# kv of two pairs of heads computed next to the q·kv of the two pairs ahead of them

## The chip, the cores and the metric

The kernel runs on one core of one Trainium2 chip. The metric is the time of one execution in microseconds (us), taken as the median of several runs. The granted clock is the share of its full clock that TensorE was given, averaged over a run.

## The reference, cut to what matters

```python
# q, k, v: (batch 8, heads 8, seq 576, head_dim 64), f32
kv  = einsum('bhsd,bhse->bhde', k, v)        # 64 x 64 for each head
out = einsum('bhsd,bhde->bhse', q, kv)
out = out / sqrt(mean(out * out, -1) + 1e-6) * g_norm
x = out.transpose(0, 2, 1, 3).reshape(4608, 512)
a, b = x @ w1, x @ w2                        # (512, 1024) each
result = ((a * b) @ w3) @ w_out              # (4608, 512)
```

## The kernel before

The kernel first folds w3 and w_out into one matrix (the first 85 us), and then runs nine groups of 512 tokens. In each, the FFN matmuls (all in a function `winograd`, 128 x 128 weights, 256 columns) fill TensorE, and the attention of the next batch is slipped in between them in pieces, at points called `between()`. There are up to eight such points, or stretches, in a group. The heads go in four pairs.

```python
inp = ctx.enter_context(tc.tile_pool(name="inp", bufs=2))          # k, v, q of two pairs
ps_at = ctx.enter_context(tc.tile_pool(name="ps_at", bufs=3, space=PSUM))
kv_sb = [const.tile([P, 2, NP, D], FP32, name=f"kv_sb{i}") for i in range(2)]
...
def kv(rs):                      # of pairs rs; one PSUM bank
    for r in rs:
        for j in range(J + 1):
            for e in range(2):   # 128 rows x 64 columns of the array
                nc.tensor.matmul(kv_ps[e * D:(e + 1) * D, r - rs[0], :], lhsT=..., rhs=..., ...)
    ...                          # four copies to kv_sb on ScalarE

def q_t(r):                      # 4 full-size transposes, one bank, one copy on ScalarE
def product(h):                  # q kv of pairs 2h, 2h+1: 64 x 64 tiles, two banks
    ...
    return norm(...)             # squares on ScalarE, sums, reciprocal and scaling on VectorE
def turn(r):                     # 4 full-size transposes of the result

def begin(*rs):
    kv(rs)
    for r in rs:
        q_t(r)
        load_pair(...)           # k, v and q of the pair two ahead

pieces = [
    [(begin, 0, 1)], [(middle, 0)], [(turn, 0), (turn, 1)],
    [(begin, 2, 3)], [(middle, 1)], [(turn, 2), (turn, 3)],
    [], [],                      # odd batches: leftover tokens of two batches
]
```

`middle(h)` is `product(h)` with its whole norm. The last 64 tokens of each batch, the leftovers, are treated two batches at a time, by `q_t_left`, `product_left` and `turn_left`.

## Time and profile before

| | before |
|---|---|
| median of the first 3 runs | 814.15 us (813.13 to 815.48) |
| span of the profiled run, granted clock | 811.6 us, 1.000 |
| TensorE / VectorE / ScalarE busy | 99% / 45% / 33% |
| TensorE's waits after 85 us | none |

The lines are shown in the prediction below. In a line of TensorE, `128*64` is the part of its array that the instruction uses, rows by columns; this is called the tile form here. TensorE's records overlap: an FFN matmul's record lasts 379 ns, and the next starts 216 ns after it. So a share of busy time says nothing of what one instruction costs on this path. Read the distance from one start to the next, and compare the same group of instructions with different neighbours.

### The profile page before, as it was taken

How to read it: one execution, taken by the hardware profiler on the slowest of the kernel's cores; microseconds unless marked ns; L12 is line 12 of the kernel's file. 1: busy time of each engine (PE TensorE's matmuls, PEld its weight loads, DVE VectorE, ACT ScalarE, POOL GpSimd, SP SyncE). 2: the span in 40 equal slices, each digit the busy share in tenths (PEclk: the TensorE clock that was granted, in tenths of full speed). 3: DMA queues.
4: the chain of work that ended last, by engine and by line, in shares of the span. 5: the costliest groups of instructions: out<-in, count | busy, mean ns of one | idle time of the engine just before them, and what ended most of it. 6: DMA issues, size and time to landing. Idle time of an engine off the chain costs nothing.

```text
span 811.6 us, 12588 instructions
## 1 busy us (share of the span) xinstructions
PE 803.0 (99%) x5335; PEld 676.8 (83%) x5335; DVE 363.6 (45%) x680; ACT 266.8 (33%) x501; POOL 1.8 (0%) x8
## 2 busy tenths in 40 slices
PE   7999999999999999999999999999999999999998
PEld 5455788888888888888888888888888888888887
DVE  6958998324522453155315531543154415422431
ACT  6677743124312431233124322331234212211220
POOL 0000000000000000000000000000000000000000
PEclk9999999999999999999999999999999999999999
DMA  9996433032003210312032202120210010002001
GB/s 322 332 328 182 146 91 92 1 131 82 10 1 130 75 31 1 119 47 56 1 103 67 66 1 85 56 82 0 79 52 1 1 52 1 0 1 53 1 0 53
DMA packets 60811, 59.53 MB, mean 73 GB/s; under 512 B 15316, under 2 KB 57300, under 8 KB 60756
## 3 DMA queue, kind: packets, MB, share of 16 engines
q1 hardware_dynamic: 60608, 58.60, 23.2%
q8 instruction: 42, 0.69, 0.4%
q14 instruction: 13, 0.11, 0.0%
q10 hardware_dynamic: 148, 0.13, 0.0%
HBM read 49.28 MB, written 9.44 MB: 72 GB/s over the span
## 4 chain that ended last, share of the span: by engine, by line
PE 98%; DMA 1%; DVE 0%; SPq 0%; ACT 0%; issue 0%; ACTq 0%
PE mm L471 81%; PE mm L456 7%; PE at L275 3%; PE at L345 2%; PE at L294 2%; PE at L378 2%; DMA raw<-in_moe_w_out_dram 1%; PE at L443 1%; PE at L363 0%; SPq L183 0%; PE at L387 0%; PE at L304 0%; DVE chunks L160 0%; DVE ab L150 0%; ACT ab L147 0%
## 5 line engine op out<-in xcount | busy, mean ns | idle before, releaser
L471 PE MATMUL mm<-xT,w_sb 128*128 128x256 f32 x768 | 176.2, 379 | 0.0
L471 PEld LDWEIGHTS mm<-xT,w_sb 128*128 128x128 f32 x768 | 146.0, 190 | 20.2 <-issue 0.5
L471 PE MATMUL mm<-xc,ws 128*128 128x256 f32 x576 | 130.2, 379 | 0.0
L471 PEld LDWEIGHTS mm<-xc,ws 128*128 128x128 f32 x576 | 109.5, 190 | 14.8
L484 ACT COPY u<-mm 128x512 f32<-128x512 f32 x90 | 52.7, 585 | 206.0 <-PE mm L471 185.9
L484 ACT COPY p<-mm 128x512 f32<-128x512 f32 x90 | 52.7, 586 | 134.4 <-PE mm L471 134.4
L471 PE MATMUL mm<-w3o_sb,ab 128*128 128x256 f32 x432 | 96.2, 379 | 0.0
L597 DVE TENSOR_TENSOR c<-mm,u 128x512 f32<-128x512 f32 x36 | 24.8, 689 | 157.3 <-PE mm L471 157.3
L471 PEld LDWEIGHTS mm<-w3o_sb,ab 128*128 128x128 f32 x432 | 82.1, 190 | 11.1
L471 PE MATMUL mm<-xc,w_sb 128*128 128x256 f32 x288 | 68.9, 382 | 0.0
L471 PE MATMUL mm<-raw 128*128 128x256 f32 x288 | 63.6, 379 | 0.0
L471 PE MATMUL mm<-xT,ws 128*128 128x256 f32 x256 | 61.6, 383 | 0.0
L471 PEld LDWEIGHTS mm<-raw 128*128 128x128 f32 x288 | 54.8, 190 | 7.4
L456 PE MATMUL mm<-chunks,ab 128*128 128x512 f32 x128 | 60.0, 601 | 0.2 <-DVE chunks L160 0.2
L471 PEld LDWEIGHTS mm<-xc,w_sb 128*128 128x128 f32 x288 | 52.8, 190 | 6.9 <-ACT u L484 0.3
L471 PEld LDWEIGHTS mm<-xT,ws 128*128 128x128 f32 x256 | 46.7, 190 | 6.0
L314 DVE TENSOR_REDUCE inv<-sq 128x8 f32<-128x512 f32 (+1 forms) x40 | 23.5, 626 | 58.4 <-ACT sq L313 58.4
L598 DVE TENSOR_TENSOR ab<-c 128x256 f32<-128x256 f32 x108 | 45.4, 421 | 2.9
L638 DVE TENSOR_TENSOR raw<-mm,u 128x512 f32<-128x512 f32 x8 | 5.5, 692 | 83.4 <-PE mm L471 72.7
L456 PEld LDWEIGHTS mm<-chunks,ab 128*128 128x128 f32 x128 | 21.9, 190 | 21.6 <-issue 16.1
L597 DVE TENSOR_TENSOR c<-p,u 128x512 f32<-128x512 f32 x36 | 24.9, 691 | 28.4 <-ACT u L484 28.1
L471 PE MATMUL mm<-w3o_sb,raw 128*128 128x256 f32 x144 | 32.7, 380 | 0.0
(90 smaller groups left out, 769.3 us busy)
## 6 DMA issues: line engine op xcount, KB each, us to landing
raw<-in_moe_w_dram SPq DMA_DIRECT2D x31, 512.0 KB, 7.0
k_sb<-in_k_dram SPq DMA_DIRECT2D x32, 256.0 KB, 3.9
v_sb<-in_v_dram SPq DMA_DIRECT2D x32, 256.0 KB, 4.4
q_sb<-in_q_dram SPq DMA_DIRECT2D x32, 256.0 KB, 4.5
out_dram<-raw SPq DMA_DIRECT2D x14, 512.0 KB, 2.6
raw<-in_moe_w_out_dram SPq DMA_DIRECT2D x7, 512.0 KB, 7.7
out_dram<-raw SPq DMA_DIRECT2D x9, 128.0 KB, 2.4
kl_sb<-in_k_dram SPq DMA_DIRECT2D x8, 128.0 KB, 4.8
```

Source lines behind the costliest of these rows:

```text
L275: nc.tensor.matmul(kv_ps[e * D:(e + 1) * D, r - rs[0], :], lhsT=k_sb[:, e, cols] if j < J else kl[:, 2 * r + e, :], rhs=v_sb[:, e, cols] i ...
L294: nc.tensor.transpose(qt_ps[:, e, i, :], q_sb[:, e, i * P:(i + 1) * P], ident)
L314: nc.vector.tensor_reduce(out=inv[:, i], in_=sq.rearrange("p (h d) -> p h d", d=D), axis=AX.X, op=ALU.add)
L345: nc.tensor.matmul(o_ps[l][tokens, n * D:(n + 1) * D], lhsT=qT[r][rows, e, i, tokens], rhs=kv_b[rows, e, r, :], start=True, stop=True,)
L378: nc.tensor.transpose(t_ps[:, j, :], st[r // 2][:, j // 2, j % 2, m:m + 2, :], ident)
L443: nc.tensor.transpose(t_ps[:, m, :], src, ident)
L456: nc.tensor.matmul(sums_ps[half][m], lhsT=w3T[half, c][:, m, :], rhs=chunks[:, c, 1, :], start=(c == 0), stop=(c == KF - 1),)
L471: nc.tensor.matmul(ps[:, u, :], lhsT=lhsT(a_name, u, c), rhs=rhs(b_name, c),  start=(u == 0 and c == 0 and to is None), stop=(c == chunks ...
L484: nc.scalar.copy(t, ps)
L597: nc.vector.tensor_add(c, one, two)
L598: nc.vector.tensor_mul(dst, c[:, 0, :], c[:, 1, :])
L638: nc.vector.tensor_add(dst, one, two)
```

## The change

The intent is to have fewer places where TensorE goes from full-size matmuls to small tiles and back. A border between two tile forms is called a seam here, and a place where kv is put directly next to a product a merge. kv(2,3) moves to the stretch of product(0), and kv(0,1) of the next batch to the stretch of product(1). As kv is now ready while the kv of two other batches is still needed (the leftovers use it), it gets a third place. Loads of k and v come apart from those of q. The core of the diff:

```diff
-    def load_pair(b, r):
+    def load_pair(names, b, r):
 ...
-        kv_b = kv_sb[b % 2]
+        kv_b = kv_sb[b % 3]
 ...
-                            rhs=kv_sb[l][rows, e, r, :],
+                            rhs=kv_sb[(b - 1 + l) % 3][rows, e, r, :],
 ...
-        def begin(*rs):
+        def begin_kv(*rs):
             kv(rs)
             for r in rs:
+                load_ahead("kv", r)
+
+        def begin_q(*rs):
+            for r in rs:
                 q_t(r)
 ...
-        pieces = [
-            [(begin, 0, 1)],
-            [(middle, 0)],
-            [(turn, 0), (turn, 1)],
-            [(begin, 2, 3)],
-            [(middle, 1)],
-            [(turn, 2), (turn, 3)],
-            [],
-            [],
-        ]
 ...
+        if b == 1:
+            fs[0].append((a.begin_kv, 0, 1))
+        fs[0].append((a.begin_q, 0, 1))
+        fs[1] += [(a.begin_kv, 2, 3), (a.finish, 0)]
+        fs[2].append((a.begin_q, 2, 3))
+        fs[3] += [(a.turn, 0), (a.turn, 1)]
+        if more:
+            fs[5].append((batch(b + 1).begin_kv, 0, 1))
+        fs[5].append((a.finish, 1))
+        fs[7] += [(a.turn, 2), (a.turn, 3)]
 ...
+    kv_sb.append(late_pool.tile([P, 2, NP, D], FP32, name="kv_sb2"))
```

More of the change, by code (lines that the diff above doesn't have):

```diff
@@ L1 @@
 from contextlib import ExitStack
+from types import SimpleNamespace
 import numpy as np
@@ L87 @@
     kv_left = [const.tile([P, H, D], FP32, name=f"{name}l_sb") for name in "kv"]
-    def load_pair(b, r):
-        tiles = []
-        for name, src in (("k", k), ("v", v), ("q", q)):
+    def load_pair(names, b, r):
+        for name in names:
             t = inp.tile([P, 2, J * D], FP32, name=f"{name}_sb")
@@ L95, in load_pair @@
                 out=t,
-                in_=src[b, 2 * r:2 * r + 2, 0:G, :].rearrange("h (p j) d -> p h (j d)", j=J),
-            )
-            tiles.append(t)
-        loaded[b, r] = tiles
+                in_=dict(k=k, v=v, q=q)[name][b, 2 * r:2 * r + 2, 0:G, :].rearrange(
+                    "h (p j) d -> p h (j d)", j=J
+                ),
+            )
+            loaded[name, b, r] = t
     def load_kv_left(b):
@@ L259, in attention, with start @@
     def attention(b):
-        kv_b = kv_sb[b % 2]
+        kv_b = kv_sb[b % 3]
         qT = {}
-        x = xT[b] = work.tile([P, 2, 2, NP // 2, N], FP32, name="xT")
+        def start():
+            xT[b] = work.tile([P, 2, 2, NP // 2, N], FP32, name="xT")
         def kv(rs):
@@ L269, in kv @@
             for r in rs:
-                k_sb, v_sb, _ = loaded[b, r]
+                k_sb, v_sb = loaded["k", b, r], loaded["v", b, r]
                 kl, vl = kv_left
@@ L288, in q_t @@
         def q_t(r):
-            q_sb = loaded[b, r][-1]
+            q_sb = loaded["q", b, r]
             qt_ps = bank(ps_at, "at").rearrange("p (e i t) -> p e i t", e=2, i=2)
@@ L378, in turn @@
                 nc.tensor.transpose(t_ps[:, j, :], st[r // 2][:, j // 2, j % 2, m:m + 2, :], ident)
-            dst = x[:, r // 2, :, r % 2, :]
+            dst = xT[b][:, r // 2, :, r % 2, :]
             nc.scalar.activation(
@@ L392, in turn_left, with load_ahead @@
             nc.scalar.activation(dst, t_ps, AF.Copy, scale=g_col)
-        def middle(h):
-            all_of(product(h))
-        def begin(*rs):
+        def load_ahead(names, r):
+            if r + 2 < NP:
+                load_pair(names, b, r + 2)
+            elif b + 1 < B:
+                load_pair(names, b + 1, r + 2 - NP)
+                if r + 1 == NP and "k" in names:
+                    load_kv_left(b + 1)
+        def begin_kv(*rs):
             kv(rs)
             for r in rs:
+                load_ahead("kv", r)
@@ L400, in begin @@
+        def begin_q(*rs):
+            for r in rs:
                 q_t(r)
-                if r + 2 < NP:
-                    load_pair(b, r + 2)
-                elif b + 1 < B:
-                    load_pair(b + 1, r + 2 - NP)
-                    if r + 1 == NP:
-                        load_kv_left(b + 1)
-                        if b == 0:
-                            load_q_left(1)
-        if b == 0:
-            return begin, product, turn
-        pieces = [
-            [(begin, 0, 1)],
-            [(middle, 0)],
-            [(turn, 0), (turn, 1)],
-            [(begin, 2, 3)],
-            [(middle, 1)],
-            [(turn, 2), (turn, 3)],
-            [],
-            [],
-        ]
@@ L422, in attention, with begin @@
-        if b % 2:
-            pieces[2].insert(0, (q_t_left,))
-            pieces[6].append((product_left,))
-            pieces[7].append((turn_left,))
-            if b + 1 < B:
-                pieces[7].append((load_q_left, b + 1))
-        elif b + 1 < B:
-            pieces[0].append((load_q_left, b + 1))
-        def steps(fs):
-            return lambda: [f(*a) for f, *a in fs]
-        return [steps(fs) for fs in pieces]
+                load_ahead("q", r)
+        def begin(r):
+            begin_kv(r)
+            begin_q(r)
@@ new lines, in finish, with batch, steps @@
+        def finish(h):
+            all_of(product(h))
+        return SimpleNamespace(**{f.__name__: f for f in (
+            start, begin_kv, begin_q, begin, product, finish, turn, q_t_left, product_left, turn_left,
+        )})
+    batches = {}
+    def batch(b):
+        if b not in batches:
+            batches[b] = attention(b)
+        return batches[b]
+    def steps(b):
+        a = batch(b)
+        a.start()
+        more = b + 1 < B
+        fs = [[] for _ in range(8)]
+        if b == 1:
[8 more added lines that the diff above has]
+        fs[7] += [(a.turn, 2), (a.turn, 3)]
+        if b % 2:
+            fs[2].insert(0, (a.q_t_left,))
+            fs[6].append((a.product_left,))
+            fs[7].append((a.turn_left,))
+            if more:
+                fs[7].append((load_q_left, b + 1))
+        elif more:
+            fs[0].append((load_q_left, b + 1))
+        return iter([lambda s=s: [f(*args) for f, *args in s] for s in fs])
@@ L686 @@
                 load_kv_left(0)
-                load_pair(0, 0)
+                load_pair("kvq", 0, 0)
             elif c == 5:
-                load_pair(0, 1)
+                load_pair("kvq", 0, 1)
                 load_q_left(0)
@@ L693 @@
             fold_chunk(0, c, [NH - 1])
-        begin, product, turn = attention(0)
+        first = batch(0)
+        first.start()
         AT = {1: 0, 2: 1, 4: 2, 5: 3}
@@ L701 @@
             if c in AT:
-                begin(AT[c])
+                first.begin(AT[c])
+                if AT[c] + 1 == NP:
+                    load_q_left(1)
             if c - 1 in norms:
@@ L721 @@
                 if AT[c] % 2:
-                    norms[c] = product(AT[c] // 2)
+                    norms[c] = first.product(AT[c] // 2)
                     next(norms[c])
@@ L725 @@
             if c - 1 in norms:
-                turn(AT[c - 1] - 1)
-                turn(AT[c - 1])
+                first.turn(AT[c - 1] - 1)
+                first.turn(AT[c - 1])
     fold_cm.__exit__(None, None, None)
@@ L730 @@
     allocate()
+    kv_sb.append(late_pool.tile([P, 2, NP, D], FP32, name="kv_sb2"))
     groups = [*range(B - 1), B, B - 1]
     for n, T in enumerate(groups):
-        pieces = iter(attention(T + 1) if n + 2 < NG else [])
+        pieces = steps(T + 1) if n + 2 < NG else iter([])
         def between():
```

## The prediction

> **What bounds the kernel now.** I read the page's busy table first, then the chain that ended last, then TensorE's list of waits, and last TensorE's timeline over part of one steady batch. In the first fence the columns of the first line are busy time, share of the span and instruction count; the second is the chain's share by engine.
>
> ```profile
> PE 803.0 (99%) x5335; PEld 676.8 (83%) x5335; DVE 363.6 (45%) x680; ACT 266.8 (33%) x501; POOL 1.8 (0%) x8
> ...
> PE 98%; DMA 1%; DVE 0%; SPq 0%; ACT 0%; issue 0%; ACTq 0%
> PE mm L471 81%; PE mm L456 7%; PE at L275 3%; PE at L345 2%; PE at L294 2%; PE at L378 2%; DMA raw<-in_moe_w_out_dram 1%; PE at L443 1%; PE at L363 0%; SPq L183 0%; PE at L387 0%; PE at L304 0%; DVE chunks L160 0%; DVE ab L150 0%; ACT ab L147 0%
> ```
>
> TensorE is the path: 98% of the chain is its own work. VectorE (45%), ScalarE (33%) and DMA are far from it. The waits of TensorE confirm it; columns are who waited for whom, total us, times, longest.
>
> ```profile
> PE at L443 <- DVE chunks L160: 2.7, 1, 2.7
> PE mm L256 <- POOL ident masks.py:199: 1.9, 1, 1.9
> PE mm L456 <- DVE chunks L160: 0.2, 1, 0.2
> ```
>
> These are 4.8 us in all, all in the first microseconds of the run. From 85 us on, TensorE waits for nobody. So only fewer or cheaper TensorE instructions can shorten the kernel, and "busy" hides what is dear in them, because overlapped records make one unbroken block. I therefore read starts, not durations. This is the timeline of TensorE for half a batch (start us, us, engine, line, operation, tiles, count):
>
> ```profile
> 255.21 0.69 PE L275 MATMUL at<-v_sb,k_sb 128*64 128x64 f32 x16
> 255.72 0.29 PE L275 MATMUL at<-vl_sb,kl_sb 128*64 128x64 f32 x4
> 255.84 0.64 PE L275 MATMUL at<-v_sb,k_sb 128*64 128x64 f32 x16
> 256.31 0.29 PE L275 MATMUL at<-vl_sb,kl_sb 128*64 128x64 f32 x4
> 256.52 1.10 PE L294 MATMUL at<-ident,q_sb 128*128 128x128 f32 x8
> 257.46 1.89 PE L471 MATMUL mm<-xT,ws 128*128 128x256 f32 x8
> 259.19 3.62 PE L471 MATMUL mm<-xT,w_sb 128*128 128x256 f32 x16
> 262.73 1.16 PE L345 MATMUL at<-kv_sb,qT 64*64 64x64 f32 x64
> 263.82 2.00 PE L471 MATMUL mm<-xc,w_sb 128*128 128x256 f32 x8
> 265.65 1.89 PE L471 MATMUL mm<-xT,w_sb 128*128 128x256 f32 x8
> 267.38 3.62 PE L471 MATMUL mm<-xc,ws 128*128 128x256 f32 x16
> 270.84 0.60 PE L304 MATMUL at<-ident,ql_sb 128*128 128x128 f32 x4
> 271.27 1.04 PE L378 MATMUL at<-ident,xn 128*128 128x128 f32 x8
> 272.15 1.89 PE L471 MATMUL mm<-xT,ws 128*128 128x256 f32 x8
> ```
>
> Take start to start. Sixteen FFN matmuls cost 270.84-267.38 = 3.46 us when a full-size transpose follows, but 262.73-259.19 = 3.54 when the 64*64 product follows: +0.09 to go into a tiled block. Eight FFN matmuls cost 267.38-265.65 = 1.73 normally, 265.65-263.82 = 1.83 right after the 64*64 block: +0.10. Eight transposes cost 272.15-271.27 = 0.88 after transposes, 257.46-256.52 = 0.94 after kv: +0.06. Inside kv, the last four matmuls cost 256.52-256.31 = 0.21 against 0.12 for the same four at 255.72: +0.09; the first sixteen cost 0.51 against 0.47: +0.04. Transposes between FFN matmuls cost nothing extra. So it is the **change of tile form** that costs, at both of its sides.
>
> **What the Trainium skill says.** "TensorEngine Tiling (Array Packing)", section "Key Properties", says that changing the tiling mode, not merely the tile, drains TensorE. The trace agrees: alternating between column halves inside kv costs nothing visible (20 matmuls of one pair in about 0.6 us), the change of form costs the 0.09 to 0.21 above. The same page lists 128x64 and 64x64 as different configurations (section "Available Configurations"), so kv next to q kv should still be one change. "Perfetto Trace Analysis", in its account of the TensorE instruction's lifecycle, says that the profiler estimates a matmul's end; hence starts here. Here too the trace agrees: records of 379 ns start every 216 ns.
>
> **The change, part by part.**
>
> *Instructions.* None of TensorE's is added or removed: 688 merged rows before and after, and the two orders hold the same matmuls. Before, a steady batch has four tiled stretches: kv(0,1), product(0), kv(2,3), product(1). After, it has two: kv(2,3)+product(0), and kv(0,1) of the next batch+product(1). The q transposes stand alone among full-size matmuls. The listing of the changed order shows the pairs: 7 batches (1 to 7) have the first, 6 (1 to 6) the second, as batch 7 has no successor. So **13 merges**. Batch 1's first kv stays with its transposes; batch 0 is untouched, and the four products of leftovers stay alone.
>
> *What a merge removes.* Single starts in the trace (before and after the seam): FFN to kv 308 ns instead of 216 (+92), first kv gap of its kind 100 instead of 52 (+48), last kv to transpose 151 instead of 52 (+99), first transpose 169 instead of 109 (+60). A lone kv block thus costs 92+48+99+60 = 299 ns of switching. A lone product costs +93 and +48 to go in, +109 and +105 to go out: 355 ns.
>
> *What it adds.* The new seam, kv to product, costs X. If it drains as the other changes do, the last kv gap grows by 99 and the first product group by 48: X = 147 ns. The rest of the pair's overhead is that of one product (in and out). So a merge saves 299 - 147 = 152 ns, and 13 save 13 x 0.152 = 1.98 us. If the seam is free, 13 x 0.299 = 3.9 us. All of it lies on the path, since TensorE waits for nobody.
>
> *What it moves.* ScalarE's four kv copies (1.07 us in all) now stand ahead of the two squares of the norm, so the norm ends up to 1.1 us later. Its readers come later too: in the steady batch q transposes that reuse its banks follow some 32 FFN matmuls later (32 x 0.216 = 6.9 us), and the norm took 4.4 us (product ended at 287.76, xn at 292.14). Loads: k and v of a batch come half a batch earlier and have about three stretches to land (over 15 us against 4 to 5 us). The third kv place costs no time.
>
> **The rivals.**
>
> *The first use in batch 1.* Its kv(0,1) and kv(2,3) are one stretch apart. In the trace k of pair 2 is issued at 103.26 when kv(0) is done, and v of pair 3, issued at 106.14 behind a q load, landed at 110.44. The new order puts the q loads behind, so I estimate 109 to 109.6 for the last v. kv(2,3) is due at about 110.05. It should just fit; missing costs under 1 us, once. Also the norm there has little room: xn ended at 117.97, its turn was due at 118.59, and VectorE was busy with weights. After, a q transpose waits for the same bank, about 1.2 us later, with a norm about 1 us later. A wait would again be a fraction of a us.
>
> *A new wait in every batch* (PSUM banks, three of them, or the tighter order on ScalarE). Against it: the 6.9 against 5.5 us above, and no wait there now. It would have to be 0.15 us per merge to eat the gain, and could reach 1 us per batch, so 821 at worst.
>
> *TensorE's seam dearer than thought*: 64*64 after 128*64 could cost as much as the two changes that it replaces. For: I have no such seam in the trace. Then nothing is won: 814.
>
> *The seam free*, as both use 64 columns: 810.3.
>
> **Range and chances.** I weigh 75% for a draining seam (1.98), 20% for a nearly free one (3.6), 5% for no gain: 1.5+0.7 = 2.2 us, less 0.1 for small waits of batch 1. 814.15 - 2.1 = 812.05, told as 812.0. The three runs of before spread from 813.13 to 815.48, over 2 us, as large as the gain, so the range must hold that noise: 810.0 to 814.2. A 2% gain would be 16 us; all switching in the steady part is 14 x 0.299 + 14 x 0.355 + 4 x 0.355 = 10.6 us, so that can't be reached: 0.5%. Slower by 2% needs a wait of 2.3 us in each of seven batches: 1%. Same: 98.5%.
>
> **What would show it.** TensorE's timeline after: kv and product adjacent 13 times, FFN matmuls of +0.09 ahead of only these, transposes of q at 0.88 instead of 0.94, and the last kv gap before the product near 150 ns (or 52: free). A steady batch shorter by 0.3 us (its period without leftovers was 81.54, from 168.40 to 249.94). TensorE's waits still empty after 85 us. The prediction is wrong if a wait on a DMA, on ScalarE's kv copies or on VectorE's xn appears there, or if the period shrinks by other than 0.3 to 0.6 us.

## More of the kernel before

The sessions ran on different chips, so a kernel is compared with the kernel before of its own session.

## The result, and the profile after

The changed kernel took **812.1 us** (median of 6 runs, 811.05 to 813.69), the kernel before 813.75 us (6 runs). The ratio is 0.9978 (95% interval 0.9963 to 0.9994): "same" at 2%, but clear of no change.

The page of the changed kernel, busy line and share of the chain by engine, and then TensorE's waits:

```profile
PE 801.9 (99%) x5335; PEld 677.6 (84%) x5335; DVE 364.6 (45%) x680; ACT 264.6 (33%) x501; POOL 1.8 (0%) x8
...
PE 98%; DMA 1%; DVE 0%; SPq 0%; ACT 0%; issue 0%; ACTq 0%
```

```profile
PE at L468 <- DVE chunks L161: 2.0, 1, 2.0
PE mm L257 <- POOL ident masks.py:199: 1.9, 1, 1.9
PE mm L481 <- DVE chunks L161: 1.5, 1, 1.5
```

The bound is the same, the instruction counts are the same, and all three waits still lie at the start. No wait came in. TensorE's timeline at the place that answers to the one in the prediction:

```profile
263.61 0.69 PE L278 MATMUL at<-v_sb,k_sb 128*64 128x64 f32 x16
264.12 0.29 PE L278 MATMUL at<-vl_sb,kl_sb 128*64 128x64 f32 x4
264.24 0.64 PE L278 MATMUL at<-v_sb,k_sb 128*64 128x64 f32 x16
264.70 0.29 PE L278 MATMUL at<-vl_sb,kl_sb 128*64 128x64 f32 x4
264.92 1.16 PE L348 MATMUL at<-kv_sb,qT 64*64 64x64 f32 x64
266.01 1.99 PE L496 MATMUL mm<-xc,w_sb 128*128 128x256 f32 x8
267.84 1.89 PE L496 MATMUL mm<-xT,w_sb 128*128 128x256 f32 x8
...
273.46 1.04 PE L297 MATMUL at<-ident,q_sb 128*128 128x128 f32 x8
274.33 1.03 PE L496 MATMUL mm<-xT,ws 128*128 128x256 f32 x4
```

kv now runs straight into the product. The last four of kv take 264.92-264.70 = 0.22 us where undisturbed ones take 264.24-264.12 = 0.12, so the seam is not free. The eight q transposes take 274.33-273.46 = 0.87 instead of 0.94. Leaving the product still costs 0.10 (267.84-266.01 = 1.83 against 1.73).

The weight loads (PEld) show that a drain fits, that is, that TensorE starts nothing of a new form before the old one has left. These are the ways into and out of a product in the kernel before:

```profile
262.73 1.02 PEld L345 LDWEIGHTS at<-kv_sb,qT 64*64 64x64 f32 x64 [0.33 <-issue]
262.73 1.16 PE L345 MATMUL at<-kv_sb,qT 64*64 64x64 f32 x64
...
263.82 0.30 PEld L471 LDWEIGHTS mm<-xc,w_sb 128*128 128x128 f32 x2
263.82 0.48 PE L471 MATMUL mm<-xc,w_sb 128*128 128x256 f32 x1
```

At every seam after 95 us, in both kernels, the first weight load of the new form starts 0 to 2 ns before its matmul (1 to 2 ns at the 13 new seams). Where only the shape changes and the form stays, it starts one matmul ahead: 213 to 215 ns from FFN matmuls to transposes, 106 to 108 ns from transposes to FFN matmuls.

The two profiled spans, 811.6 and 811.1, differ by only 0.5 us. That is misleading, because the start of the two runs differs. So I use a measure that leaves the start out: from the first kv of batch 1 to the start of the last 16 FFN matmuls, called **the steady part** below. First the kernel before, then the changed one (timeline of TensorE):

```profile
102.53 0.69 PE L275 MATMUL at<-v_sb,k_sb 128*64 128x64 f32 x16
...
804.28 3.62 PE L471 MATMUL mm<-raw,ab 128*128 128x256 f32 x16
```

```profile
104.01 0.69 PE L278 MATMUL at<-v_sb,k_sb 128*64 128x64 f32 x16
...
803.79 3.62 PE L496 MATMUL mm<-raw,ab 128*128 128x256 f32 x16
```

Before, it is 804.28-102.53 = 701.75 us; after, 803.79-104.01 = 699.78. The gain is **1.97 us**, or 1.97/13 = 0.152 for each of the 13 merges. The rest of the difference is in the first 20 us, which the first experiment takes up.

### The profile page after: what moved, and what is told of

Same layout as the page of the kernel before. It is cut to its first block, busy times and chain, and to the rows that moved or that the text cites. A ratio compares the mean times of both kernels' runs of the same rounds, so it can differ in the third digit from the quotient of the medians.

```text
span 811.1 us, 12622 instructions
## 1 busy us (share of the span) xinstructions
PE 801.9 (99%) x5335; PEld 677.6 (84%) x5335; DVE 364.6 (45%) x680; ACT 264.6 (33%) x501; POOL 1.8 (0%) x8
## 4 chain that ended last, share of the span: by engine, by line
PE 98%; DMA 1%; DVE 0%; SPq 0%; ACT 0%; issue 0%; ACTq 0%
PE mm L496 81%; PE mm L481 7%; PE at L278 3%; PE at L348 2%; PE at L297 2%; PE at L381 2%; PE at L468 1%; DMA raw<-in_moe_w_out_dram 1%; PE at L366 0%; SPq L184 0%; PE at L307 0%; PE at L390 0%; DVE chunks L161 0%; DVE ab L151 0%; ACT ab L148 0%
```

## The experiments

Each kernel was built on the changed one unless said otherwise, and each result was correct. From before_warm down, each also has the dummy matmuls that are explained next, and the kernel before beside it does not, so these ratios hold what the dummies bring too. In the table, "before FFN" is the start of the first FFN matmul, "first tokens" from there to the first kv of batch 1, "steady" the steady part. The three columns are of the profiled run, the medians of all fast runs. The medians of the kernel before on the same chip are beside them.

| kernel | before FFN | first tokens | steady | median us | kernel before | ratio (95%) |
|---|---|---|---|---|---|---|
| before | 85.04 | 17.50 | 701.75 | | 813.75 | |
| the change | 86.50 | 17.51 | 699.78 | 812.1 | 813.75 | 0.9978 (0.9963 to 0.9994) |
| before_warm | 85.11 | 18.44 | 701.74 | 813.47 | 814.93 | 0.9984 (0.9971 to 0.9998) |
| after_warm | 85.08 | 17.49 | 699.78 | 811.98 | 814.93 | 0.9965 (0.9952 to 0.9977) |
| first_seam | 85.10 | 17.82 | 701.55 | 813.29 | 814.11 | 0.9988 (0.9972 to 1.0004) |
| between | 84.44 | 17.75 | 703.29 | 814.9 | 814.11 | 1.0007 (0.9992 to 1.0022) |
| apart | 84.94 | 17.55 | 702.14 | 814.24 | 814.11 | 0.9998 (0.9983 to 1.0013) |
| swap | 85.44 | 17.75 | 699.78 | 812.05 | 814.11 | 0.9968 (0.9951 to 0.9985) |
| four_kv | 85.22 | 17.45 | 698.74 | 810.55 | 814.88 | 0.9947 (0.9935 to 0.996) |
| four_kv_exits | 85.03 | 17.71 | 704.16 | 816.43 | 814.88 | 1.0019 (1.0006 to 1.0033) |
| after_again | 85.27 | 17.51 | 699.78 | 811.67 | 814.88 | 0.996 (0.9947 to 0.9972) |
| exits_late | 85.35 | 17.56 | 698.30 | 810.07 | 813.88 | 0.9948 (0.9936 to 0.996) |
| four_kv_again | 84.90 | 17.36 | 698.74 | 810.78 | 813.88 | 0.9958 (0.9945 to 0.9971) |

The steady part repeats to 0.01 us: 701.75 and 701.74 for the old order, 699.78 four times with 13 seams, 698.74 twice. The expectations below were written for "first tokens" and "steady" together (719.24 before, 717.29 after). "First tokens" scatters by up to 1 us between runs of one order (17.50 and 18.44): there the last weights are still being converted, and in before_warm TensorE waited 0.7 us for a ScalarE copy. So I read the verdicts from the steady part.

### The start: before_warm and after_warm

The theory was that the scatter of the runs is TensorE's clock. The Trainium skill ("TensorE: Matmul & The Clock Gate", section "Part 1: The HAM clock gate") says that a free-running window of 3413 ns with an idle TensorE halves its clock. Below are two adjacent windows of the kernel before and two of the changed kernel (us; length; busy time and count of TensorE, weight loads, VectorE, ScalarE, GpSimd; granted clock; DMA share; GB/s):

```profile
10.51:13.92 3.41, 2.01 (x5) 0.57 (x3) 2.51 (x3) 2.82 (x4) 0.00 (x0) 1.00 1.06 382
13.93:17.33 3.40, 2.09 (x8) 1.18 (x9) 3.33 (x4) 2.66 (x4) 0.00 (x0) 1.00 1.05 372
```

```profile
11.82:15.23 3.41, 1.44 (x5) 0.37 (x4) 3.34 (x5) 2.66 (x4) 0.00 (x0) 1.00 1.07 375
15.24:18.64 3.40, 3.40 (x8) 1.83 (x8) 3.33 (x4) 2.48 (x3) 0.00 (x0) 0.50 1.08 380
```

In the changed kernel's run TensorE was busy for 1.44 of 3.41 us, and the next window ran at 0.50. In the run of before, a longer wait (2.73 us against 1.97) was split over two windows of 2.01 and 2.09, and the clock stayed at 1.00. FFN work then began at 86.50 instead of 85.04. The experiment fills the gap with ten dummy matmuls, in both kernels:

```diff
             fold_chunk(0, c, range(NH - 1))
+            if c == 0:
+                keep_warm(10)
             turn_w3(*((0, c + 1) if c + 1 < KF else (1, 0)))
```

> The kernel before with ten dummy identity matmuls (about 2.1 us of TensorE work) put into TensorE's idle time after the first three fold matmuls, nothing else. Theory (the scatter of the runs is TensorE's granted clock: in the profiled run of the change one window of 3.413 us, from 15.23 to 18.65, ran at half clock after TensorE had stood nearly idle from 11.9 to 15.1, and FFN work began 1.46 us later than in the kernel before): all runs at clock 1.000 and within 0.6 us of one another, at 813.1 to 813.5. Rival (the scatter is the DMA of the weights): scatter of 2 us stays, and the clock does not go with it.

> The changed kernel with the same ten dummy matmuls. Theory (13 seams, each 147 to 151 ns in place of 299): its runs fall to 811.0 to 811.4, 2.0 us under before_warm, with no run near 812.9, and the part of the trace from the first FFN matmul to the end is the same as in the changed kernel. Rival (the measured gain of 1.65 us in medians is partly chance of the start): the difference to before_warm is other than 1.7 to 2.3 us.

All ten runs had a clock of 0.999 or 1.000, and they lay within 1.24 us (813.16 to 814.4) and 0.77 us (811.49 to 812.26). In the same session 7 of the 9 runs of the plain kernel before had 0.997 or 0.998. In the last session it ran at 0.999 or 1.000 seven times (mean 813.51) and at 0.998 four times (mean 815.11): 1.6 us apart. Over all four sessions it is 15 runs with a mean of 813.68 against 21 with 815.05, 1.4 us apart. In the session of these two kernels it is only 0.8, and one run at 0.997 (813.85) was faster than both at 1.000. So the theory holds for a part of the scatter; up to 1.24 us is left without it, more than the 0.6 that I had expected, and its cause is not shown. All five runs of after_warm also lie above the expected 811.0 to 811.4. The difference of the two means, 813.66-811.91 = 1.75 us, agrees with the 1.97 of the trace within the scatter; that of the medians, 1.49, is outside the expected 1.7 to 2.3. The dummies stay in all the kernels that follow; four_kv_exits aside, 47 of the 48 runs with them had 0.999 or 1.000.

### Is it the form change? Three ways of undoing it

**first_seam** keeps only the seven merges of kv(2,3) with product(0). kv(0,1) goes back to its own q transposes, so nothing is half a batch ahead any more.

```diff
-        if b == 1:
-            fs[0].append((a.begin_kv, 0, 1))
+        fs[0].append((a.begin_kv, 0, 1))
 ...
-        if more:
-            fs[5].append((batch(b + 1).begin_kv, 0, 1))
         fs[5].append((a.finish, 1))
```

> Only the first kind of merge: kv(2,3) ahead of product(0), 7 times; kv(0,1) stays with its own q transposes, so nothing is computed half a batch ahead. With the ten dummy matmuls at the start. Read from the first FFN matmul's start to the start of the last 16 FFN matmuls, which took 719.24 us in the kernel before and 717.29 in the changed one. Theory (299 - 151 = 148 ns a merge): six merges fewer than the change, 717.28 + 6 x 0.148 = 718.2 us; 7 last kv gaps of 151 before a product, 7 before a transpose. Rival (the third place of kv and the earlier loads bring the gain): 719.2, or 717.3 if only the moved q transposes count.

The steady part is 701.55, hardly better than before. On the wider measure of the expectation it is 719.37: a miss of the theory's 718.2, and near the rival's 719.2. But TensorE's timeline shows one wait that neither had foreseen:

```profile
263.33 0.29 PE L278 MATMUL at<-vl_sb,kl_sb 128*64 128x64 f32 x4
264.26 0.69 PE L278 MATMUL at<-v_sb,k_sb 128*64 128x64 f32 x16 [0.64 <-DMA v_sb<-in_v_dram]
```

Between the two kv halves 264.26-263.33 = 0.93 us went by instead of 0.12, for a load of v. That block of kv lasted 2.171 us, the six others 1.315. Without this 0.856 the steady part is 700.69, and 701.75-700.69 = 1.06 = 7 x 0.151: the seven merges. This correction was made afterwards. The single starts need none: the last kv gap is 151 to 152 ns before a product 7 times and 152 to 153 before a transpose 7 times, as the theory said. So there are seven merges' gains without any look-ahead; apart, below, tests the rival (the look-ahead brings the gain) from the other side. What the look-ahead does bring shows here too: without it kv(2,3) follows its loads after one stretch, and one of seven came late.

**between** leaves everything in the stretch where the change has put it, and puts one full-size transpose of the identity between kv and product:

```diff
+            if n == 2:
+                nc.tensor.transpose(kv_bank[:, 2 * P:3 * P], ident, ident)
```

> The changed kernel (dummy matmuls at the start) with one full-size transpose, of the identity into an unused part of the kv bank, between each kv of two pairs and what follows it: everything stays half a batch ahead, the blocks stay in the same stretch, but the tile form now changes twice more, at 13 places. Theory: the last kv gap stays 151, the transpose costs 109 + about 60, and going from it into the 64*64 product costs 0 to 93 on top, plus 48: 717.28 + 14 x 0.109 + 13 x (0.06 to 0.15) = 719.6 to 720.8 us. Rival (only being in one stretch counts, not the form): the transposes' own 14 x 0.109, 718.8.

```profile
182.29 0.29 PE L279 MATMUL at<-vl_sb,kl_sb 128*64 128x64 f32 x4
182.51 0.33 PE L287 MATMUL at<-ident 128*128 128x128 f32 x1
182.77 1.16 PE L351 MATMUL at<-kv_sb,qT 64*64 64x64 f32 x64
```

kv still needs 182.51-182.29 = 0.22 for its last four, and the lone transpose takes 182.77-182.51 = 0.26 instead of 0.11, as it pays for both of its sides. The steady part rose by 703.29-699.78 = 3.51 us. The 13 lone transposes at 258 ns are 3.35, and the 14th, which stands with other transposes, 0.11; together 3.46. That is at the upper end of the theory, whose range was 2.3 to 3.5 (on the wider measure 721.03, 0.2 over its 720.8), and far beyond the rival's 1.5. Being in one stretch does not help if the form changes inside it.

**apart** keeps the look-ahead, the third place and the loads, and takes 12 of the 13 kv away from the product: six stand alone among FFN matmuls, six right behind q transposes.

```diff
-        fs[1] += [(a.begin_kv, 2, 3), (a.finish, 0)]
+        fs[0 if b > 1 else 1].append((a.begin_kv, 2, 3))
+        fs[1].append((a.finish, 0))
 ...
-            fs[5].append((batch(b + 1).begin_kv, 0, 1))
+            fs[4].append((batch(b + 1).begin_kv, 0, 1))
```

> The changed kernel (dummy matmuls at the start) with kv still computed ahead, in three places, with the same loads, but in stretches of its own: kv(0,1) of the next batch one stretch before product(1), and kv(2,3) of batches 2 to 7 right after the q transposes of pairs 0 and 1. 12 of 13 merges undone, 1 left. Theory: a kv alone among FFN matmuls costs 92+48+109+105 = 354 instead of 151 (+203, six times), a kv between transposes and FFN costs 48+214 and Y = 0 to 92 for going in (+111 to +203, six times): 717.28 + 1.9 to 2.4 = 719.2 to 719.7 us, no better than the kernel before. Rival (the gain comes from the look-ahead): 717.3.

```profile
174.90 1.04 PE L297 MATMUL at<-ident,q_sb 128*128 128x128 f32 x8
175.87 0.69 PE L278 MATMUL at<-v_sb,k_sb 128*64 128x64 f32 x16
...
177.19 1.99 PE L497 MATMUL mm<-xT,ws 128*128 128x256 f32 x8
179.01 3.62 PE L497 MATMUL mm<-xT,w_sb 128*128 128x256 f32 x16
```

The eight transposes ahead of kv take 175.87-174.90 = 0.97, 0.10 more than among FFN matmuls; the FFN matmuls after it 179.01-177.19 = 1.82, 0.09 more than 1.73. The steady part is 702.14, 2.36 us over the change (0.197 for each of 12) and 0.39 over the kernel before. So the order before was better than "ahead but apart", since it let kv go out into transposes, which is cheaper. On the wider measure it is 719.68, within the theory's 719.2 to 719.7 and far from the rival's 717.3. The look-ahead alone wins nothing; the gain is that of the adjacency.

### Does the direction matter? swap

```diff
-        fs[1] += [(a.begin_kv, 2, 3), (a.finish, 0)]
+        fs[1] += [(a.finish, 0), (a.begin_kv, 2, 3)]
```

and the same at the second place.

> The changed kernel (dummy matmuls at the start) with the product ahead of kv in each of the 13 pairs. Theory (a form change costs the same in both directions, and going out to FFN matmuls costs 214 ns from either): 717.3 us, as before the swap. Rival (the seam is cheap because the product's 64-row weights are quick to load): the seam to kv or the way out of kv differs by over 30 ns, 13 times, 717.7 or more, or 716.9 or less.

The steady part is 699.78, the same to 0.01 us. (The 717.53 of the wider measure holds 0.26 of "first tokens".) The single starts read 148 ns for the last product gap ahead of kv, where 39 is usual: +109 in place of kv's +100. Going out from kv, the last gap is 152 instead of 52, and the first FFN gap 320 instead of 216. What one end loses the other wins, and both differ by 10 ns, where the rival asked for over 30.

### Two ways further: four_kv, four_kv_exits, exits_late

**four_kv** follows the reason to its end: all four pairs' kv of the next batch stand with product(1), which leaves 6 seams, and product(0) stands alone. k and v need four places each, 8 KB a partition more. I made room by letting the squares of the norm use xn as scratch, and by giving xn one place. The core of the edit:

```diff
-        fs[1] += [(a.begin_kv, 2, 3), (a.finish, 0)]
+        fs[1].append((a.finish, 0))
 ...
-            fs[5].append((batch(b + 1).begin_kv, 0, 1))
+            fs[5].append((batch(b + 1).begin_kv, *range(NP)))
 ...
-                sq = work.tile([P, G], FP32, name="sq")[:, 0:w]
+                sq = scratch[:, i * w:(i + 1) * w]
```

> All four pairs' kv of the next batch in one stretch with product(1) of this one; product(0) stands alone. k and v have places for four pairs; to make room the squares of the norm go into xn before it is overwritten, and xn has one place. With the ten dummy matmuls. Theory: seven seams of 151 ns fewer than in the change (6 left): 717.27 - 7 x 0.151 = 716.2 us from the first FFN matmul to the last 16, no new wait of TensorE, time 1.06 us under after_again. Rival (the longer block or the single xn brings a wait on ScalarE's copies, on VectorE or on a load): 717 or more, and the waits show which.

The steady part fell to 698.74, by 1.04 (7 seams of 0.149), and TensorE waits nowhere after the start. The time was 810.55 us, against 811.67 of after_again in the same session: 1.12 less, where 1.06 was expected.

> The changed kernel with the ten dummy matmuls once more, as the measure for the two others on the same chip: 717.27 us from the first FFN matmul to the last 16 within 0.3, clock 0.999 to 1.000 in all runs.

**four_kv_exits** moves one group of transposes behind each lone product (7 of product(0), 4 of the leftovers, whose place in the stretch moves too), so that the way out of the small tiles leads to transposes and not to FFN matmuls.

```diff
-        fs[1].append((a.finish, 0))
-        fs[2].append((a.begin_q, 2, 3))
+        fs[1] += [(a.finish, 0), (a.begin_q, 2)]
+        fs[2].append((a.begin_q, 3))
 ...
-        fs[7] += [(a.turn, 2), (a.turn, 3)]
+        fs[6 if b % 2 else 7].append((a.turn, 2))
+        fs[7].append((a.turn, 3))
```

> As four_kv, and after product(0) and after the product of leftovers one group of four transposes that was in the next stretch (q of pair 2; xn of pair 2): 11 times the way out of the 64*64 form goes to transposes. Theory (what a change costs depends on what comes after: 109+105 to FFN matmuls of 216 ns, 99+60 to transposes of 109 ns): 55 ns fewer 11 times, 716.2 - 0.6 = 715.6 us. Rival (the drain is the product's own): 716.2, or more where the transposes wait for a bank or for xn.

It missed, at 816.43 us, slower than the kernel before. TensorE's waits and the window of the clock just after that wait tell why:

```profile
PE at L300 <- DMA q_sb<-in_q_dram: 4.3, 1, 4.3
```

```profile
116.73:120.13 3.40, 3.27 (x10) 2.85 (x11) 2.15 (x6) 0.79 (x2) 0.00 (x0) 0.50 0.28 78
```

In batch 1, q of pair 2 was now needed one stretch after its load, and the load was the 11th behind ten of k and v: it was issued at 110.08 and landed at 116.73. TensorE waited 4.3 us, and the idle time brought one window of half clock (1.57 us more). A single load in a single batch undid more than everything else had won. **exits_late** leaves only that one transpose group where it was:

```diff
-        fs[1] += [(a.finish, 0), (a.begin_q, 2)]
+        fs[1].append((a.finish, 0))
+        fs[1 if b > 1 else 2].append((a.begin_q, 2))
```

> As four_kv_exits, but batch 1 keeps both q transposes of pairs 2 and 3 in the later stretch, so that its q load, the 11th of a queue of k and v loads, has 12 more FFN products' time to land; ten early ways out remain. Theory (four_kv_exits lost 4.34 us to that one load and 1.57 us to the window of half clock that the idle time brought): 716.19 - 10 x 0.055 = 715.6 us from the first FFN matmul to the last 16, no wait on a load, time 0.55 us under four_kv_again and about 1.6 under after_again, near 810.0. Rival (earlier transposes wait elsewhere): a wait of TensorE on a load, on ScalarE or on VectorE, and 716.2 or more.

> four_kv once more, as the measure for exits_late on the same chip: 716.19 us within 0.3, no wait.

```profile
263.28 1.16 PE L351 MATMUL at<-kv_sb,qT 64*64 64x64 f32 x64
264.37 0.66 PE L300 MATMUL at<-ident,q_sb 128*128 128x128 f32 x4
264.87 1.89 PE L511 MATMUL mm<-xc,w_sb 128*128 128x256 f32 x8
```

The four transposes take 264.87-264.37 = 0.50 instead of 0.44: the way out costs 0.06 on this side, not the 0.10 of FFN matmuls. The steady part is 698.30, 0.44 under four_kv for ten exits (0.044 each, where I had put 0.055). The time is 810.07 us, the lowest of all; four_kv_again had 810.78 (one of its six runs at clock 0.998). The intervals of the two against the kernel before overlap, so that exits_late beats four_kv is shown by the trace, not by the times. Against the kernel before it is 0.9948 (0.9936 to 0.996). A part of that is the dummies, which the kernel before lacks: before_warm, which has nothing else, had 0.9984.

## Why the prediction was right

- **The bound.** TensorE alone, no wait after 85 us: so it stayed.
- **13 merges.** The trace has 13 products right after kv and one kv before transposes.
- **The seam.** It was weighed at 75% that it drains like the others, X = 147 ns. Read singly, the last kv gap before a product is 151 to 152 ns (52 usual, +99) and the first product group 87 (39 usual, +48): 147. By the prediction's sum a merge saves 152, and 13 save 1.98; measured 1.97. One term was read a little high: 169 ns for the first transpose after kv is the most of 14 (164 to 169, mean 166), and with the mean it is 149 and 1.94. The free seam and the seam without any gain both fall.
- **812.0 us.** Measured 812.1. The digit is luck: the gain in medians was 1.65 against 2.1 foretold, and the kernel before came to 813.75 in six runs, not 814.15; the two misses of 0.4 us cancel. The chance of a window of half clock moves a run by about 1.4 us, and it hit three of the six runs of the changed kernel (812.9, 812.89 and 813.69, at 0.997 or 0.998), while the first three of before that I started from were not told apart by clock.
- **The norm later by up to 1.1 us.** Too much. ScalarE copied kv from 265.04 to 266.11, while the product still ran (264.92 to 266.01), and the squares began at 266.14, 0.13 after the product; before, 0.12 after. xn ended 4.51 us after the product; before, 4.65 (batch 3 in both).
- **The first use in batch 1.** Just fitted, as expected, though closer: the last v landed at 111.57, and kv of pair 3 started at 112.17. This start is 1.48 us later than before, so the estimate of 109 to 109.6 would have been 110.5 to 111.1, and the landing was another 0.5 to 1.1 later. first_seam and four_kv_exits show what happens where it doesn't fit.
- **A steady batch shorter by 0.3 us.** From 171.04 to 252.28 it is 81.24, against 81.54.
- **Two slips without weight.** The prediction's "0.09 to 0.21 above" for a change of form doesn't fit its own lines, which give 0.04 to 0.10 for one side; 0.21 is reached only with both sides of product to FFN (109+105 ns). Its 688 merged rows stand in no view of the record; the traces have 5335 matmul records before and after.

## What to carry to other kernels

On a TensorE that never waits, list the places where the tile form changes, take the cost of each side from start-to-start gaps in the trace, and put blocks of small tiles next to each other: each block saved that way was worth 0.15 us here. Then look at what the new order asks of the loads in the first batch, where they have the least lead; one late load of 4.3 us cost more than 13 saved changes. Compare kernels by a stretch of the trace that leaves the start out, and look at the granted clock of each run: here it differed between runs of the same kernel, and their mean time with it by 1.4 us.

## What the Trainium skill lacked or had wrong

- "TensorEngine Tiling (Array Packing)", section "Key Properties", says that a change of tiling mode drains TensorE, without a size. The runs fit that (the first weight load of a new form starts 0 to 2 ns before its matmul, instead of one matmul ahead) and give the sizes, by the neighbours (last gap plus first gap over the usual): FFN matmuls to kv +92 and +48 ns, to 64 x 64 products +93 and +48; kv to product +99 and +48; product to kv +109 and +48; kv to transposes +100 and +57; product to FFN matmuls +109 and +105; kv to FFN matmuls +100 and +104.
- No page says that full-size f32 transposes among full-size matmuls cost next to nothing extra (27 times in the changed kernel the last gap is 215 to 216 ns before them and 109 to 110 inside them, as usual, and the first FFN gap after them 218 to 219), nor that leaving small tiles into transposes is cheaper than into FFN matmuls (by 44 ns for each of ten exits).
- "TensorE: Matmul & The Clock Gate", section "Part 1: The HAM clock gate", says that the clock drops after an idle window and that the window is free-running. The lengths agree (3.413 us at 0.50), but the window before it need not be idle throughout: here TensorE's records filled 1.44 of 3.41 us. Windows filled to 1.94 us (same run, from 8.41), 2.01 and 2.09 us did no harm, though the last two held a wait of 2.73 us. In four_kv_exits the window before was idle throughout (no TensorE record from 112.90 to 116.71), as the page has it.
